# Attention, a squared-ReLU layer and a gated layer in one kernel: new numbers and rules for the planner that writes the order of the instructions

## The chip, the cores and the metric

The kernel runs on one core of a Trainium2 chip. Its time is the device time of one execution in microseconds (us), the median of several runs. One further execution was taken by the hardware profiler; all rows below are from it.

## The reference

Three layers follow each other, on 8 batches of 576 positions, 8 heads of 64 columns and 32 memory slots; the two feed-forward layers see 4608 tokens of 512 columns with 2048 hidden columns.

```python
# 1: attention through 32 slots
a = softmax(phi, axis=slots)                       # (b, h, s, 32), maximum subtracted
k_m = einsum('bhsm,bhsd->bhmd', a, k);  v_m = einsum('bhsm,bhsd->bhmd', a, v)
attn = softmax(q @ k_m.T / sqrt(64))               # (b, h, s, 32)
x = concat_heads(attn @ v_m)                       # 4608 x 512
# 2: first layer
r = maximum(x @ w_in, 0);  x = (s * r * r + b) @ w_out
# 3: second layer
h = x @ w1;  g = h * sigmoid(1.702 * h);  out = g @ w2
```

All is float32. The first weight matrix is not applied to x: `v_m @ w_in` is formed for each batch, 32 slots by 2048 columns per head, and attn is multiplied with that.

## The kernel before, in words

**Stages.** A plan lists the work in four stages. Stage 1, for each batch b: the slots of two groups of four heads (`slots`, written for g = 0 and 1), their attention weights (`attend`), four products of the slot values with a quarter of w_in (`matrix`, j = 0 to 3), and for each quarter four `step`s of twelve matmuls, each 128 x 288, whose ReLU goes to DRAM as r. Stage 2 multiplies the squares of r with w_out, one sequence s (a batch) after the other (`down` with "wo"). Stage 3 multiplies with w1 and gates (`up`), stage 4 multiplies with w2 (`down` with "w2"). Stages 2 to 4 use the seven-product scheme for 2 x 2 blocks: seven passes (numbers 1, 2, 6, 7, 5, 3, 4 in that order) accumulate in three PSUM tiles X, Y and Z, and sums and differences are formed on VectorE.

**Two halves.** Every operand of a matmul is split into a high part (a rounded copy) and a low part (the operand minus the copy), and three matmuls stand for one: high by high, high by low, low by high (lines 258 to 260, 602 to 604, 707 to 709). A high part is a copy on ScalarE or VectorE (lines 234 and 235); a low part is a subtraction on VectorE (line 239, shared by all such operations, so the tile names tell them apart: `ml` for `matrix`, `al` for attention weights, `ol` for stages 2 to 4).

**Weights** come as 64-bit floats. `convert` loads 512 KB (`raw`) and rebuilds a 32-bit number: two operations on ScalarE or VectorE (lines 278 to 287), three on VectorE (293 to 295: clamp, shift, sign), one addition on GpSimd (298). `prepare` does so for a quarter q of w_out, w1 or w2, forms the seven operands, splits each and stores it to DRAM; `weights` loads it when its stage comes. These stores and loads are called `w` in the trace's names.

**The maximum over the slots** in `slots` needs a path through three engines: VectorE reduces (line 404), TensorE transposes (412), VectorE reduces again to `nm` (413), TensorE transposes back (414), VectorE subtracts (409), ScalarE takes the exponential (416), TensorE multiplies with the keys and values (430, 432), VectorE normalizes to `an` (439 to 441), TensorE transposes it (447).

**The order** is not written by hand. Each operation is recorded with a due time, its possible engines with a cost in us, and the tiles it reads and writes. `Order.sort` is a list scheduler: at each turn it computes for every ready operation (among those due at most AHEAD after the most urgent one) when it could start: when its engine is free in the plan and its inputs were produced, plus LAG if on another engine. Each engine takes the earliest candidate, the due time deciding between equals, and the whole picks the earliest of the engines. The result is one fixed list per engine; at run time each engine goes through its list in order and waits on semaphores. All DMAs stand in the list of SyncE (SP). Wrong costs in the plan therefore do no harm to the results, only to the order. The relevant numbers are `LAG, FILL, AHEAD = 0.2, 2.5, 90.0` (line 36), `COL = 0.4527` ns for each column of a matmul (line 172), and B1, B2, the due-time length of a batch of stage 1 and of a sequence of the later stages (174). While the first batch is prepared, extra matmuls on an identity matrix (`warm`, line 747) fill the idle time that the plan sees on TensorE.

Of the kernel before, what the change touches and what calls it, by code (L numbers as in the profile page):

```python
# [27 lines left out]
class Order:  # L28
# [7 lines left out]
    LAG, FILL, AHEAD = 0.2, 2.5, 90.0  # L36
    WEIGHT = {"dve": 1.0, "pool": 1.6, "act": 1.0}

    def __init__(self, bufs):
        self.bufs, self.ops, self.fill = bufs, [], None  # L40
        self.wrote, self.read, self.users = {}, {}, {}

    def add(self, due, ways, r=(), w=()):
# [16 lines left out]
        self.ops.append((due, ways, deps, new))  # L60

    def sort(self):
        ops = self.ops
# [17 lines left out]
        ready = sorted((ops[n][0], n) for n in range(len(ops)) if not left[n])  # L81
        since = {n: 0.0 for _, n in ready}
        while ready:
            can = {}
            limit = ready[0][0] + self.AHEAD
            for due, n in ready:
# [32 lines left out]
            t, due, n, i = min(first)  # L119
            _, ways, _, new = ops[n]  # L120
            eng, cost, fn = ways[i]
# [7 lines left out]
            ready.remove((due, n))  # L129
            out.append(fn)  # L130
            for m in after[n]:
                left[m] -= 1
                if not left[m]:
                    bisect.insort(ready, (ops[m][0], m))
            for x in of[n]:
                last[x] = max(last[x], end[n])
                uses[x] -= 1
                if not uses[x]:
                    heapq.heappush(free[x[0]], last[x] + self.LAG)
# [5 lines left out]
class Net:  # L145
# [26 lines left out]
    COL = 0.4527  # L172

    B1, B2 = 38.5, 43.9
# [40 lines left out]
    def act(self, n, fn, psum=False, count=1):  # L215
        return "act", count * ((166 if psum else 195) + 0.835 * n) / 1e3, fn

    def dve(self, n, fn, fast=False, count=1):
        return "dve", count * (120 + (0.6 if fast else 1.06) * n) / 1e3, fn

    def pool(self, n, fn, fast=False):
        return "pool", (160 + (0.9 if fast else 2.6) * n) / 1e3, fn

    def pe(self, due, n, fn, r=(), w=()):
        self.order.add(due, [("pe", self.COL * n / 1e3, fn)], r, w)

    def dma(self, due, out, in_, r=(), w=(), kb=288):

        self.order.add(due, [("sync", kb / 340, lambda: self.nc.sync.dma_start(out(), in_()))], r, w)

    def hi(self, due, n, out, src, r, w, psum=False):
# [3 lines left out]
                             self.dve(n, lambda: nc.vector.tensor_copy(out(), src()), fast=not psum)], r, w)  # L235

    def tt(self, due, n, out, a, b, op, r, w, pool=False):
        nc = self.nc
        ways = [self.dve(n, lambda: nc.vector.tensor_tensor(out(), a(), b(), op=op))]  # L239
        if pool:  # L240
            ways.append(self.pool(n, lambda: nc.gpsimd.tensor_tensor(out(), a(), b(), op=op)))
        self.order.add(due, ways, r, w)

    def lo(self, due, n, out, src, hi, r, w, pool=False):

        self.tt(due, n, out, src, lambda: hi().bitcast(F32), ALU.subtract, r, w, pool)

    def on_act(self, due, n, fn, r=(), w=(), **k):
        self.order.add(due, [self.act(n, fn, **k)], r, w)

    def on_dve(self, due, n, fn, r=(), w=(), **k):
        self.order.add(due, [self.dve(n, fn, **k)], r, w)
# [10 lines left out]
    def convert(self, due, key, out, src, lead=6):  # L263
# [25 lines left out]
        def b():  # L289
            H, m = T[raw][:, :, 1], to["m"]  # L290
            mf = m.bitcast(F32)
            v = nc.vector
            v.tensor_scalar(mf, mf, bits(0x38000000), bits(0x47EFFFFF), op0=ALU.max, op1=ALU.min)
            v.tensor_scalar(m, m, 3, 0x3FFFFFF8, op0=ALU.logical_shift_left, op1=ALU.bitwise_and)
            v.scalar_tensor_tensor(m, H, 0xC0000000, m, op0=ALU.bitwise_and, op1=ALU.bitwise_or)
# [5 lines left out]
        for f, r, w in ((size, (*raw, 1), key), (low, (*raw, 1), (*raw, 0))):  # L301
            self.order.add(due, [self.act(512, lambda f=f: f(True)), self.dve(512, lambda f=f: f(False), fast=True)], (r,), (w,))
        self.on_dve(due, 512, b, ((*raw, 1),), (key,), fast=True, count=4)
        self.order.add(due, [("pool", 1.45, c)], ((*raw, 0),), (key,))
# [89 lines left out]
    def slots(self, b, g, due):  # L394
# [6 lines left out]
        self.dma(d - 8, lambda: self.t(ph, [P, 4, 5, 32]), lambda: self.a["phi"][b, g], (), (ph,), 320)  # L401
# [32 lines left out]
        self.pe(d + 4, 3600, mm, (ph, *fs, f1), (z,))  # L434
# [19 lines left out]
    def attend(self, b, g, due):  # L454
# [37 lines left out]
        self.on_dve(d + 2, S, lambda: with_slots(nc.vector, sm, ALU.subtract), (sm,), (st,))  # L492
        self.on_act(d + 3, S, lambda: nc.scalar.activation(T[st], T[st], AF.Exp, scale=0.125), (), (st,))
        self.on_dve(d + 4, S + 200, total, (st,), (sm2,))
        self.on_dve(d + 4, S, lambda: with_slots(nc.vector, sm2, ALU.mult), (sm2,), (st,))
# [6 lines left out]
    def matrix(self, b, j, due):  # L502
# [14 lines left out]
        self.pe(due, 5200, mm, (*kms, *[(*w, c) for w in ws for c in range(2)]), (pm,))  # L517
# [92 lines left out]
    def leave(self, name, s, i, z, due, X, Y, Z):  # L610
# [5 lines left out]

        def copy(k, half):

            if not scaled:
                self.on_act(due, n, lambda: nc.scalar.copy(self.two(k), T[X][:, :, 0:HS]), (X,), (k,), psum=True)  # L620
                return
            for o in range(2):
# [5 lines left out]
                self.on_act(due, HS + 100, f, (X, ("bw", 0), ("sc", 0, 0), *(((*k, 0),) if o else ())), ((*k, o),), psum=True)  # L628
# [266 lines left out]
```

## Time and profile before

| | us |
|---|---|
| median of 3 runs | 1498.03 (1495.05 to 1500.3) |
| the profiled execution | 1494.7 |
| its span, first to last instruction | 1492.9 |
| TensorE busy | 1414.1 (95%) |
| VectorE busy | 1198.5 (80%) |
| ScalarE busy | 775.0 (52%) |
| GpSimd busy | 96.2 (6%) |

Busy times are sums over the whole span; where the idle time of TensorE lies is read from a table by stretches of time, and what it waited for from the groups of instructions and from the timeline. TensorE's matmuls overlap: a 128 x 288 matmul is shown with about 0.3 us and the next one starts 0.13 us later. "PEclk" is the granted clock of TensorE as a share of 2.4 GHz.

### The profile page before, as it was taken

What the parts mean: (1) busy time and instruction counts of PE and PEld (TensorE: products, weight loads), DVE (VectorE), ACT (ScalarE), POOL (GpSimd) and SP (SyncE); (2) the same over time, 40 slices, a digit from 0 to 9 for tenths busy, and PEclk for the clock granted to TensorE, in tenths of its full rate; (3) what the DMA queues carried; (4) which work ended last, traced back from release to release, by engine and by line L of the source; (5) the groups of instructions that cost most, each with busy time, mean ns of one, the idle gap of its engine ahead of it and who ended that gap; (6) DMA issues with size and microseconds to landing.
All of it is one profiled execution on the core that took longest, in us unless ns stands there. A gap on an engine that the chain in (4) does not pass through costs nothing.

```text
span 1492.9 us, 28830 instructions
## 1 busy us (share of the span) xinstructions
PE 1414.1 (95%) x11192; PEld 1350.1 (90%) x11192; DVE 1198.5 (80%) x1836; ACT 775.0 (52%) x1244; POOL 96.2 (6%) x70
## 2 busy tenths in 40 slices
PE   7598899889999999999999999999999999999998
PEld 5476677767998999999999999999999999999998
DVE  6869888686799998998868888797649887778882
ACT  5345554436677767676545565564446433344431
POOL 1401110000101010100010101010000000000000
PEclk8699999999999999999999999999999999999999
DMA  9778988659885637564696575656389445444330
GB/s 349 241 249 297 346 307 309 237 183 339 319 289 184 218 125 261 186 234 156 211 353 227 190 268 189 252 186 236 117 311 363 143 124 152 144 143 127 108 117 32
DMA packets 136776, 329.20 MB, mean 221 GB/s; under 512 B 15552, under 2 KB 15552, under 8 KB 136640
## 3 DMA queue, kind: packets, MB, share of 16 engines
q1 hardware_dynamic: 136640, 327.37, 63.4%
q8 instruction: 88, 1.44, 0.4%
q14 instruction: 48, 0.39, 0.1%
HBM read 192.56 MB, written 134.74 MB: 219 GB/s over the span
## 4 chain that ended last, share of the span: by engine, by line
PE 57%; ACT 0%; DMA 0%; DVE 0%; issue 0%; SPq 0%
PE X L602 6%; PE X L604 6%; PE X L603 6%; PE X L707 5%; PE X L709 5%; PE X L708 5%; PE Y L602 3%; PE Y L604 3%; PE Y L603 3%; PE Y L707 2%; PE Y L709 2%; PE Y L708 2%; PE Z L602 2%; PE Z L604 2%; PE Z L603 2%; PE Z L707 1%
## 5 line engine op out<-in xcount | busy, mean ns | idle before, releaser
L260 PE MATMUL h<-ah,ml 128*128 128x288 f32 x512 | 156.1, 305 | 22.2 <-DVE ml L239 22.2
L258 PE MATMUL h<-ah,mh 128*128 128x288 f32 x512 | 162.5, 317 | 5.5 <-ACT mh L234 3.3
L602 PE MATMUL X<-oh,wo 128*128 128x288 f32 x512 | 153.7, 300 | 10.8 <-ACT u L626 9.0
L603 PE MATMUL X<-ol,wo 128*128 128x288 f32 x512 | 152.9, 299 | 2.6 <-DVE ol L239 2.6
L259 PE MATMUL h<-al,mh 128*128 128x288 f32 x512 | 155.3, 303 | 0.0
L602 PE MATMUL X<-oh,w 128*128 128x288 f32 x512 | 151.8, 296 | 0.7 <-ACT u L620 0.7
L604 PE MATMUL X<-oh,wo 128*128 128x288 f32 x512 | 151.9, 297 | 0.0
L707 PE MATMUL X<-oh,w 128*128 128x288 f32 x512 | 151.6, 296 | 0.0
L603 PE MATMUL X<-ol,w 128*128 128x288 f32 x512 | 151.0, 295 | 0.0
L708 PE MATMUL X<-ol,w 128*128 128x288 f32 x512 | 151.0, 295 | 0.0
L604 PE MATMUL X<-oh,w 128*128 128x288 f32 x512 | 150.5, 294 | 0.0
L709 PE MATMUL X<-oh,w 128*128 128x288 f32 x512 | 150.5, 294 | 0.0
L538 ACT ACTIVATE r<-h 128x576 f32<-128x576 f32 x121 | 78.3, 650 | 114.6 <-PE h L260 104.2
L258 PEld LDWEIGHTS h<-ah,mh 128*128 128x128 f32 x512 | 101.0, 197 | 27.2 <-issue 12.0
L260 PEld LDWEIGHTS h<-ah,ml 128*128 128x128 f32 x512 | 100.6, 196 | 24.4 <-DVE ml L239 24.4
L239 DVE TENSOR_TENSOR ol<-C,oh 128x576 fp32r<-128x576 f32 x128 | 96.3, 763 | 19.7 <-PE Y L603 9.6
L239 DVE TENSOR_TENSOR ol<-A,oh 128x576 fp32r<-128x576 f32 x128 | 97.4, 778 | 15.6 <-PE Y L603 8.0
L602 PEld LDWEIGHTS X<-oh,wo 128*128 128x128 f32 x512 | 97.3, 190 | 12.9 <-ACT u L626 10.8
L259 PEld LDWEIGHTS h<-al,mh 128*128 128x128 f32 x512 | 100.9, 197 | 0.0
L603 PEld LDWEIGHTS X<-ol,wo 128*128 128x128 f32 x512 | 97.4, 190 | 3.7 <-DVE ol L239 3.7
L604 PEld LDWEIGHTS X<-oh,wo 128*128 128x128 f32 x512 | 97.7, 191 | 0.0
L602 PEld LDWEIGHTS X<-oh,w 128*128 128x128 f32 x512 | 95.9, 187 | 1.2 <-ACT u L620 1.0
(183 smaller groups left out, 4251.0 us busy)
## 6 DMA issues: line engine op xcount, KB each, us to landing
w<-w SPq DMA_DIRECT2D x112, 512.0 KB, 5.1
r<-r SPq DMA_DIRECT2D x128, 288.0 KB, 3.6
g<-g SPq DMA_DIRECT2D x128, 288.0 KB, 2.4
wo<-wo SPq DMA_DIRECT2D x42, 512.0 KB, 5.0
kv<-in_kv SPq DMA_DIRECT2D x64, 258.0 KB, 4.9
raw<-in_w SPq DMA_DIRECT2D x32, 512.0 KB, 6.0
q<-in_q SPq DMA_DIRECT2D x32, 288.0 KB, 5.2
A<-r SPq DMA_DIRECT2D x32, 288.0 KB, 3.3
```

Of the source, the lines that this page charges most:

```text
L239: ways = [self.dve(n, lambda: nc.vector.tensor_tensor(out(), a(), b(), op=op))]
L258: self.nc.tensor.matmul(ps, wh, xh, start=start and i == 0, stop=False)
L259: self.nc.tensor.matmul(ps, wh, xl, start=False, stop=False)
L260: self.nc.tensor.matmul(ps, wl, xh, start=False, stop=(i == n - 1))
L538: self.act(2 * HS, lambda: nc.scalar.activation(self.two(r), T[h][:, :, 0:HS], AF.Relu), psum=True),
L602: nc.tensor.matmul(out, T[w][:, 0, c], T[h][:, p], start=f, stop=False, skip_group_check=True)
L603: nc.tensor.matmul(out, T[w][:, 0, c], T[l][:, p], start=False, stop=False, skip_group_check=True)
L604: nc.tensor.matmul(out, T[w][:, 1, c], T[h][:, p], start=False, stop=last, skip_group_check=True)
L707: nc.tensor.matmul(out, T[w][:, 0, c], T[h][:, k], start=f, stop=False, skip_group_check=True)
L708: nc.tensor.matmul(out, T[w][:, 0, c], T[l][:, k], start=False, stop=False, skip_group_check=True)
L709: nc.tensor.matmul(out, T[w][:, 1, c], T[h][:, k], start=False, stop=k == 1, skip_group_check=True)
```

## The change

- LAG, one number before, is now one for each receiving engine: 0.7 us before TensorE may start on another engine's output, 2.5 us when the receiver is a DMA, 0.25 us for the other three.
- Costs carry a flag for the port that VectorE and GpSimd share: while a flagged operation of the one runs in the plan, no flagged operation of the other may start. All GpSimd work and VectorE's operations between SBUF tiles are flagged. The three bit operations of `convert` become three separate entries.
- The cost of a column goes from 0.4527 to 0.463 ns; the costs of the matmuls in `slots`, `attend` and `matrix` are cut (3600 to 3000, 3000 to 2200, 5200 to 2600 columns). B2 goes from 43.9 to 44.8.
- AHEAD goes from 90 to 190. In stage 1 an engine takes the most urgent of the candidates that start within 0.3 us of the earliest (SLACK).
- The operations that read X, Y or Z out in stages 2 and 4 are ranked 100 us earlier than their due time (FIRST).
- `matrix` is due 8 us before its quarter instead of 4. The first slots, the first w_in pieces and their loads get other due times, so that the first loads interleave.
- The four quarters of w1 are prepared every 115 us instead of every 65 us.

No operation of the computation is added or removed.

```diff
-    LAG, FILL, AHEAD = 0.2, 2.5, 90.0
+    FILL, AHEAD, SLACK = 2.5, 190.0, 0.3
+    LAG = {"pe": 0.7, "sync": 2.5, "dve": 0.25, "act": 0.25, "pool": 0.25}
...
+        self.rank.append(due - first)
...
-                for i, (eng, cost, _) in enumerate(ways):
+                for i, (eng, cost, _, port) in enumerate(ways):
                     t = max(t0, at.get(eng, 0.0))
+                    if port:
+                        t = max(t, held["dve" if eng == "pool" else "pool"])
                     for d in deps:
-                        e = end[d] + (self.LAG if on[d] != eng else 0.05)
+                        e = end[d] + (self.LAG[eng] if on[d] != eng else 0.05)
...
-                first.append(min((c for c in v if c[0] <= t0), key=lambda c: c[1:]))
+                first.append(min((c for c in v if c[0] <= t0 + (self.SLACK if c[1] < self.until else 0.0)), key=lambda c: c[1:]))
...
+            if port:
+                held[eng] = t + cost
...
-    COL = 0.4527
+    COL = 0.463
+    FIRST = 100
-    B1, B2 = 38.5, 43.9
+    B1, B2 = 38.5, 44.8
...
-        self.pe(d + 4, 3600, mm, (ph, *fs, f1), (z,))
+        self.pe(d + 4, 3000, mm, (ph, *fs, f1), (z,))
...
-        self.pe(d, 3000, score, (*qs, km), (ps,))
+        self.pe(d, 2200, score, (*qs, km), (ps,))
...
-        self.pe(due, 5200, mm, (*kms, *[(*w, c) for w in ws for c in range(2)]), (pm,))
+        self.pe(due, 2600, mm, (*kms, *[(*w, c) for w in ws for c in range(2)]), (pm,))
...
-                    self.slots(0, g, -40 + 5 * g)
-                    self.attend(0, g, -26 + 5 * g)
+                    self.slots(0, g, -42 + 4 * g, 10)
+                    self.attend(0, g, -28 + 4 * g)
...
-                self.matrix(b, j, d - 4)
+                self.matrix(b, j, d - 8)
...
-            self.prepare("w1", q, t2 + 10 + 65 * q, step=4)
+            self.prepare("w1", q, t2 + 10 + 115 * q, step=4)
```

What this does to the lists is shown at three places. The first is VectorE's list in the first batch, up to `ml_436`, the low part of the first `matrix` (`raw` and `wi` belong to conversions of w_in, `st`, `a`, `aT`, `ah` and `al` to the attention weights). Before:

```order
L293 TENSOR_SCALAR wi_295<-wi_295 128x512
L294 TENSOR_SCALAR wi_295<-wi_295 128x512
L295 SCALAR_TENSOR_TENSOR wi_295<-raw_280,wi_295 128x512
L293 TENSOR_SCALAR wi_310<-wi_310 128x512
L294 TENSOR_SCALAR wi_310<-wi_310 128x512
L295 SCALAR_TENSOR_TENSOR wi_310<-raw_287,wi_310 128x512
L239 TENSOR_TENSOR ml_436<-vw_372,mh_393 128x1024
```

The same place now (the low part is `ml_404`; lines are numbered by the changed file, where 247 is the old 239):

```order
L505 STREAM_TRANSPOSE aT_383<-st_313 128x576
L242 CAST ah_387<-aT_383 128x576
L247 TENSOR_TENSOR al_391<-aT_383,ah_387 128x576
L299 TENSOR_SCALAR wi_289<-wi_289 128x512
L302 SCALAR_TENSOR_TENSOR wi_289<-raw_249,wi_289 128x512
L296 TENSOR_SCALAR wi_289<-wi_289 128x512
L247 TENSOR_TENSOR ml_404<-vw_299,mh_323 128x1024
```

The first `ml` stood at row 61 of VectorE's list behind nine finished conversions of w_in, and stands at row 55 behind five finished ones and the clamp of a sixth. Four of those five now stand ahead of the first attention weights, where before only the first operation of one stood.

The second place is TensorE's list around the two transposes of the slot maximum in a later batch (`s<-ident,an` is the first, `s<-ident,nm` the second). Before:

```order
L260 MATMUL h_1503<-ah_971,ml_1400 128x288
L412 MATMUL s_1526<-ident,an_1135 128x128
L414 MATMUL s_1545<-ident,nm_1539 128x128
L515 MATMUL vw_1553<-wi_277,km_1132 32x512 x2
L515 MATMUL vw_1553<-wi_295,km_1132 32x512 x2
```

Now (first rows of it):

```order
L421 MATMUL s_1512<-ident,an_1128 128x128
L263 MATMUL h_1524<-ah_1381,mh_1444 128x288
L264 MATMUL h_1524<-al_1385,mh_1444 128x288
L265 MATMUL h_1524<-ah_1381,ml_1508 128x288
L263 MATMUL h_1524<-ah_1491,mh_1444 128x288
```

The second transpose, which stood right behind the first at four places of stage 1, now stands 24 matmuls of two steps behind it here, and at least one `vw` product behind it everywhere after the first batch. In the same list the first step that uses a `matrix` stood 12 matmuls behind it in 24 of 32 cases and 48 in seven; now it is 36 or 48 in 28 cases, while the first four cases, all in the first batch, have 0, 0, 0 and 12 (before 0, 12, 12, 12).

The third place is SP's list where stage 3 begins. `w_6_3` is the DRAM copy of piece 6 of quarter 3 of w1, `w_3_3` that of piece 3; `w_1722` and `w_1736` are the tiles that TensorE reads; `g` are stores of stage 3's output, `w_4_0` belongs to w2. Now:

```order
L236 DMA w_6_3_9740<-w_1689_9584 128x1024
L236 DMA w_4_0_9758<-w_1681_9538 128x1024
L236 DMA g_2_1_1_9779<-g_9714 128x576
L236 DMA w_1722_9799<-w_6_3_9740 128x1024
L236 DMA g_2_0_1_9820<-g_9734 128x576
L236 DMA w_3_3_9825<-w_1713_9738 128x1024
L236 DMA g_2_1_0_9834<-g_9776 128x576
L236 DMA g_3_0_0_9855<-g_9805 128x576
L236 DMA w_1736_9873<-w_3_3_9825 128x1024
```

Before, the same two pieces were stored at rows 492 and 497 of this list and loaded at rows 567 and 575; now they are stored at rows 584 and 589 and loaded at 587 and 592. The number at a name's end counts tiles in the order of the plan. Between the store 9740 and the first matmul on `w_1722` TensorE's list has some four blocks of twelve matmuls, and about as many between the store 9825 and the first on `w_1736`. For piece 7 it is seven blocks.

## Rows read from the trace of the kernel before

**Rows 1.** Stretches: length; busy PE, PEld, DVE, ACT, POOL; PEclk; DMA share; GB/s.

```profile
0.00:49.90 49.90, 29.39 (x257) 22.21 (x257) 36.96 (x64) 24.66 (x40) 13.74 (x15) 0.79 0.94 326
49.90:90.00 40.10, 33.65 (x313) 27.30 (x314) 32.40 (x53) 14.80 (x22) 9.66 (x8) 0.88 0.79 273
90.00:375.00 285.00, 252.75 (x2467) 206.81 (x2465) 227.08 (x385) 140.47 (x218) 22.21 (x16) 0.97 0.80 280
375.00:720.00 345.00, 330.55 (x2408) 326.81 (x2407) 309.50 (x459) 236.79 (x396) 25.62 (x16) 0.98 0.64 220
720.00:1488.00 768.00, 767.27 (x5753) 766.80 (x5752) 591.78 (x878) 358.27 (x568) 24.95 (x16) 1.00 0.55 189
```

**Rows 2.** Timeline, VectorE, first 50 us: start, duration, instruction, idle time before.

```profile
18.34 0.43 DVE L280 TENSOR_SCALAR wi<-raw 128x512 uint32<-128x512 uint32 x1 [2.26 <-DMA raw<-in_wi]
18.69 0.84 DVE L478 STREAM_TRANSPOSE st<-a 128x288 f32<-128x288 f32 x2
...
35.20 0.36 DVE L293 TENSOR_SCALAR wi<-wi 128x512 f32<-128x512 f32 x1
...
37.33 1.51 DVE L293 TENSOR_SCALAR wi<-wi 128x512 f32<-128x512 f32 x1
...
48.62 1.22 DVE L239 TENSOR_TENSOR ml<-vw,mh 128x1024 fp32r<-128x1024 f32 x1
```

**Rows 3.** Timeline, GpSimd, same stretch.

```profile
36.88 1.68 POOL L298 TENSOR_TENSOR wi<-wi,raw 128x512 uint32<-128x512 uint32 x1 [1.94 <-DVE wi L295]
```

**Rows 4.** Timeline, TensorE, the first low part.

```profile
49.90 0.61 PE L260 MATMUL h<-ah,ml 128*128 128x288 f32 x1 [11.74 <-DVE ml L239]
```

**Rows 5.** Groups on TensorE, 90 to 375 us: busy, mean ns, idle before and releaser.

```profile
L258 PE MATMUL h<-ah,mh 128*128 128x288 f32 x432 | 135.9, 314 | 4.4 <-ACT mh L234 2.2 <-ACT r L538 1.2 <-DVE ml L239 1.0
L260 PE MATMUL h<-ah,ml 128*128 128x288 f32 x431 | 130.0, 302 | 8.6 <-DVE ml L239 8.6
...
L515 PE MATMUL vw<-wi,km 64*32 64x512 f32 x448 | 31.9, 626 | 0.0
L472 PE MATMUL a<-q,km 64*32 64x288 f32 x192 | 13.9, 405 | 0.0
L430 PE MATMUL s<-kv,ph 128*32 128x129 f32 x384 | 13.1, 276 | 0.0
...
L447 PE MATMUL s<-ident,an 128*128 128x128 f32 x12 | 3.5, 295 | 4.3 <-DVE an L441 4.3
L414 PE MATMUL s<-ident,nm 128*128 128x128 f32 x12 | 3.5, 292 | 14.9 <-DVE nm L413 14.9
```

**Rows 6.** Timeline, TensorE, a `vw` and a slot product.

```profile
156.60 1.09 PE L515 MATMUL vw<-wi,km 64*32 64x512 f32 x16
157.62 1.09 PE L430 MATMUL s<-kv,ph 128*32 128x129 f32 x32
...
158.99 0.40 PE L258 MATMUL h<-ah,mh 128*128 128x288 f32 x1
```

**Rows 7.** Timeline, TensorE, after a long wait for `nm`.

```profile
140.60 0.29 PE L414 MATMUL s<-ident,nm 128*128 128x128 f32 x1 [4.17 <-DVE nm L413]
...
142.40 0.44 PE L259 MATMUL h<-al,mh 128*128 128x288 f32 x1
142.64 0.44 PE L260 MATMUL h<-ah,ml 128*128 128x288 f32 x1
```

**Rows 8.** Groups on VectorE, 90 to 720 us.

```profile
L239 DVE TENSOR_TENSOR ml<-vw,mh 128x1024 fp32r<-128x1024 f32 x28 | 34.1, 1216 | 9.7 <-ACT mh L234 9.4
```

**Rows 9.** Groups on ScalarE, 90 to 720 us.

```profile
L234 ACT CAST mh<-vw 128x1024 fp32r<-128x1024 f32 x24 | 24.2, 1010 | 6.2 <-PE vw L515 6.2
```

**Rows 10.** Groups on TensorE, 375 to 720 us.

```profile
L602 PE MATMUL X<-oh,wo 128*128 128x288 f32 x451 | 135.7, 301 | 10.8 <-ACT u L626 9.0 <-ACT a L626 1.6
L603 PE MATMUL X<-ol,wo 128*128 128x288 f32 x451 | 134.9, 299 | 2.6 <-DVE ol L239 2.6
```

**Rows 11.** DMA issues: count, KB each, median us to landing.

```profile
w<-w SPq DMA_DIRECT2D x112, 512.0 KB, 5.1
```

More of the change, by code (lines that the diff above doesn't have):

```diff
@@ L28, with add @@
 class Order:
[L36 removed]
+    FILL, AHEAD, SLACK = 2.5, 190.0, 0.3
+    LAG = {"pe": 0.7, "sync": 2.5, "dve": 0.25, "act": 0.25, "pool": 0.25}
     WEIGHT = {"dve": 1.0, "pool": 1.6, "act": 1.0}
     def __init__(self, bufs):
[L40 removed]
+        self.bufs, self.ops, self.rank, self.fill, self.until = bufs, [], [], None, 0
         self.wrote, self.read, self.users = {}, {}, {}
[L43 removed]
+    def add(self, due, ways, r=(), w=(), first=0):
         n = len(self.ops)
@@ L80, in sort @@
                 of[n].append(x)
-        ready = sorted((ops[n][0], n) for n in range(len(ops)) if not left[n])
+        held = {"dve": 0.0, "pool": 0.0}
+        ready = sorted((rank[n], n) for n in range(len(ops)) if not left[n])
         since = {n: 0.0 for _, n in ready}
@@ L117, in sort @@
                 t0 = min(v)[0]
-                first.append(min((c for c in v if c[0] <= t0), key=lambda c: c[1:]))
-            t, due, n, i = min(first)
+                first.append(min((c for c in v if c[0] <= t0 + (self.SLACK if c[1] < self.until else 0.0)), key=lambda c: c[1:]))
+            t, _, n, i = min(first)
             _, ways, _, new = ops[n]
-            eng, cost, fn = ways[i]
+            eng, cost, fn, port = ways[i]
+            if port:
+                held[eng] = t + cost
             if self.fill and eng == "pe":
@@ L234, in hi, with tt, lo, on_act @@
         self.order.add(due, [self.act(n, lambda: nc.scalar.copy(out(), src()), psum),
-                             self.dve(n, lambda: nc.vector.tensor_copy(out(), src()), fast=not psum)], r, w)
-    def tt(self, due, n, out, a, b, op, r, w, pool=False):
+                             self.dve(n, lambda: nc.vector.tensor_copy(out(), src()), fast=not psum, port=not psum)], r, w)
+    def tt(self, due, n, out, a, b, op, r, w, first=0):
         nc = self.nc
[L239 to L252, printed above, removed]
+        port = not any(k[0] == "ps" for k in r)
+        self.order.add(due, [self.dve(n, lambda: nc.vector.tensor_tensor(out(), a(), b(), op=op), port=port)], r, w, first)
+    def lo(self, due, n, out, src, hi, r, w):
+        self.tt(due, n, out, src, lambda: hi().bitcast(F32), ALU.subtract, r, w)
+    def on_act(self, due, n, fn, r=(), w=(), first=0, **k):
+        self.order.add(due, [self.act(n, fn, **k)], r, w, first)
+    def on_dve(self, due, n, fn, r=(), w=(), first=0, **k):
+        self.order.add(due, [self.dve(n, fn, **k)], r, w, first)
     def mm3(self, ps, pairs, start=True):
@@ L301, in convert @@
         for f, r, w in ((size, (*raw, 1), key), (low, (*raw, 1), (*raw, 0))):
-            self.order.add(due, [self.act(512, lambda f=f: f(True)), self.dve(512, lambda f=f: f(False), fast=True)], (r,), (w,))
-        self.on_dve(due, 512, b, ((*raw, 1),), (key,), fast=True, count=4)
-        self.order.add(due, [("pool", 1.45, c)], ((*raw, 0),), (key,))
+            self.order.add(due, [self.act(512, lambda f=f: f(True)), self.dve(512, lambda f=f: f(False), fast=True, port=True)], (r,), (w,))
+        self.on_dve(due, 512, clamp, (), (key,), fast=True, port=True)
+        self.on_dve(due, 512, shift, (), (key,), fast=True, port=True)
+        self.on_dve(due, 512, sign, ((*raw, 1),), (key,), port=True)
+        self.order.add(due, [("pool", 1.35, c, True)], ((*raw, 0),), (key,))
     def prepare(self, name, q, due, keep=False, step=1.5):
@@ L615, in leave @@
         scaled = name == "wo"
+        first = self.FIRST
         def copy(k, half):
             if not scaled:
-                self.on_act(due, n, lambda: nc.scalar.copy(self.two(k), T[X][:, :, 0:HS]), (X,), (k,), psum=True)
+                self.on_act(due, n, lambda: nc.scalar.copy(self.two(k), T[X][:, :, 0:HS]), (X,), (k,), first, psum=True)
                 return
@@ L764, in plan @@
         t2 = B * B1
+        self.order.until = t2
         t3, t4 = t2 + B * B2, t2 + 2 * B * B2
```

50 lines of the change are left out of this document (24 added, 26 removed).

## The prediction

> **What bounds the kernel now.** I read the table by stretches first, with one question: where is TensorE not at its full rate? From 720 us to the end it starts 5753 matmuls in 768 us, one every 0.1335 us, at PEclk 1.00 [rows 1]. Nearly all of them are 128 x 288, so 0.1335 us is the price of one such matmul, and nothing can be won there without removing matmuls. Every loss lies ahead of 720 us:
>
> - 0 to 49.9 us, the preparation of the first batch. TensorE's own work is small here. VectorE is busy 37.0 of 49.9 us [rows 1]. The stretch ends when the first low part `ml` is there: TensorE had waited 11.74 us for it [rows 4], and VectorE only began it at 48.62 us [rows 2].
> - 90 to 375 us, stage 1 from its second batch on, 285 us. Work at the full rate: 3 x 432 matmuls x 0.1335 = 173 us (three lines of this count); 28 `vw` products of 16 instructions at 1.02 us (the distance of their starts) = 28.6; 12 slot products at 1.37 = 16.4; at most 13.9 for the scores; some 4 for 36 transposes, an estimate [rows 5, 6]. That is 236 us, so 49 us are lost. The groups show 32.2 us of them as waits: 14.9 for `nm`, 4.3 for `an`, 13.0 ahead of the `h` matmuls, 11.8 of these for `mh` and `ml` [rows 5]. The rest is slow running: PEclk is 0.97 [rows 1], and after a wait of 4.17 us the matmuls start 0.24 us apart instead of 0.13, which is the lower of the two clock levels [rows 7].
> - 375 to 720 us, the end of stage 1 and most of stage 2: 2408 matmuls x 0.1335 = 321.5 of 345 us, so 23.5 us are lost [rows 1]; 13.4 are shown as waits ahead of X's matmuls, 10.8 of them for the copy that empties X on ScalarE [rows 10].
>
> VectorE is no bound over the whole span, but it is near one: 227 of 285 us (80%) in the second stretch, 309.5 of 345 (90%) in the third [rows 1].
>
> **The change part by part.** The sum is made against the profiled execution: span 1492.9, time 1494.7. The median of the runs is 1498.0, 3.3 above it.
>
> *(a) The first batch: -6.* Four conversions now stand ahead of the first attention weights, where VectorE had been waiting for data until 18.34 us [rows 2]. At most VectorE's 12.9 us of idle time come back. Against this, the loads of q stand behind four more pieces of 512 KB: at the 326 GB/s of this stretch [rows 1] that is 6.4 us later for the attention weights, which began at 18.69 us [rows 2]. The port rule helps too: a clamp of 0.36 us took 1.51 when it started behind a running GpSimd addition of 1.68 [rows 2, 3]. I take 9 us back. Then the second and third `matrix` have no matmuls left between themselves and their first user where they had twelve: 2 x 12 x 0.1335 = 3.2 us of cover gone. Bounds: -12.9 and +6.4.
>
> *(b) Stage 1 from the second batch: -28.* At four places the two transposes of the slot maximum stood back to back, so TensorE waited for VectorE to reach the reduction in its list; these make up the 14.9 us. After each some twelve matmuls run at the low clock, 12 x (0.24 - 0.1335) = 1.3 us, so 20 us in all. Now a `vw` (1.02 us) or at least a step of twelve matmuls (1.6 us) stands between. Five places have only the `vw`; I leave them 0.5 us each: -17.5. For `mh` and `ml`: a copy takes 1.01 us and the subtraction 1.22 [rows 8, 9], 2.2 us without handoffs, against 12 x 0.1335 = 1.6 us of cover before and 36 x 0.1335 = 4.8 us now. What is left over, 2.6 us, is what VectorE may be behind. Of the 11.8 us I let 1.3 stay: -10.5. The waits for `an` (4.3) keep their distances and stay. VectorE's work is the same, 227 us; in 257 us it fills 88%, near to the 90% at which the third stretch runs. Bounds: -46, all but 3 us of the loss gone and VectorE 95% full; -8, half of what the four transposes cost given back later.
>
> *(c) Stage 2: -4.* The copies of X are ranked earlier, the distances to matmuls are larger in the plan, and a quarter of w1's preparation leaves the stage. But VectorE remains at about 90%, and TensorE's list now has five places in stage 2 where the next pass into X stands directly behind the last one, where it had three. Bounds: -15 (the 13.4 us and some slow clock) and +8 (the 10.8 us grow as the places do, by five thirds).
>
> *(d) Where stage 3 begins: +5.* This is a new wait. The last quarter of w1 is prepared 150 us later, and its pieces are loaded directly behind their own stores. A transfer `w` of 512 KB takes 5.1 us to land [rows 11], so a store and the load behind it take 10.2 us. For pieces 6 and 3 four blocks of twelve matmuls cover 6.4 us of that. Piece 6 comes 3.8 us late; that delay covers piece 3, and 1.3 us go to the low clock. On SP both loads hold up what is queued behind them, stores of `g` and a store for w2, which nobody needs soon. Bounds: 0 (the stores land faster with fewer transfers around them) and +36 (the third rival).
>
> The Trainium skill ("DMA: Bandwidth & Descriptors", section "Anatomy of one DMA — SWDGE (gpsimd) path") gives a transfer 2.0 us plus its bytes at 436 GB/s, fitted on another issuing path than SP's: 3.2 us for 512 KB as an estimate, where this trace has 5.1. By that rule store and load take 6.4 us, all covered, (d) is 0 and the sum five lower; I go by the row.
>
> From 720 us on nothing is to be had, and the late part of the preparation falls where VectorE has room: 592 of 768 us [rows 1].
>
> Sum: -6 - 28 - 4 + 5 = -33; 1494.7 - 33 = 1461.7, say 1462.
>
> **The rivals.**
>
> *VectorE's list sets stage 1.* Then a wait that is removed at one transpose turns up at the next operation that VectorE is late with. For it: 90% in the third stretch goes with 23.5 us of loss on TensorE. Against it: in the second stretch it idles 58 of 285 us. Price: (b) is -12 and (c) -2: 1494.7 - 6 - 12 - 2 + 5 = 1480.
>
> *Nearly all goes.* (a) -12, (b) -46, (c) -15, (d) 0: 1422. For it: every listed wait is one of distance, and work is there to fill it. Against it: VectorE would have to run 95% full.
>
> *Slower: the last quarter of w1 comes late, one piece after the other.* Pieces 7, 6, 5 and 3 are each stored and loaded close together, and SP takes them in order, so a load that waits for its store holds up the next store. If all four chains run in series, 4 x 10.2 = 41 us, less 3 x 24 matmuls (9.6 us) between their users, plus four times 1.3 us of low clock: +36. With (b) at -8, (a) -6, (c) -4 the time is 1513. It decides once (d) is over 38 us with the other terms as forecast, or over 18 with these. Against it: pieces 7 and 5 have more cover, seven blocks for piece 7.
>
> *The plan is only permuted.* The order is another one, but its errors against the chip are as large elsewhere: within 4.5 us of before.
>
> **How the numbers follow.** Forecast 0.60, VectorE's list 0.17, nearly all 0.12, permuted 0.05, slower 0.06. A measurement tells about 0.3% (4.5 us) from no change. Faster: 0.60 + 0.17 + 0.12 = 0.89; same 0.05; slower 0.06. The range reaches from the middle between the second rival and the forecast's own low side, 1434, to 1487, above the first rival's 1480. The forecast's own range is 1445 to 1474.
>
> **What the profile will show.** (a) The first matmul on `ml` at about 43 us instead of 49.9. (b) The idle time before the second transpose under 4 us in all, that for `ml` and `mh` after the first batch under 4 us, and PEclk at 0.99 in that stretch; VectorE at 87% or more. (c) The wait for the copies of X still at 6 to 10 us. (d) One or two waits of TensorE for a transfer of `w` when stage 3 begins, some 4 us. The forecast is wrong if stage 1 from its second batch to its last `h` is less than 15 us shorter, if the waits reappear behind other operations of VectorE, or if TensorE waits over 15 us for w1.

## The result and the profile after

The changed kernel takes 1441.27 us (median of four runs, 1438.53 to 1444.89); the kernel before, on the same chip, 1496.76 (four runs). The ratio is 0.9628, 95% interval [0.9597, 0.9658]: 3.7% faster, where 2.4% were forecast (1462). The profiled execution took 1444.89, 49.8 us less than the one of before. I cut both traces at two events: the first `h` matmul of the second batch (all of the first batch lies ahead of it) and the last `h<-ah,mh` matmul (stage 1 ends).

| stretch, us | before | after | change |
|---|---|---|---|
| start to the second batch's first `h` | 97.0 | 83.1 | -14.0 |
| from there to the last `h` | 292.6 | 256.9 | -35.7 |
| from there to the end of the span | 1103.3 | 1103.1 | -0.2 |

All of the gain is in stage 1. The same stretches as [rows 1], with the columns named there, shifted to where the same work now stands:

```profile
0.00:38.15 38.15, 24.90 (x255) 20.09 (x255) 28.96 (x58) 18.51 (x29) 7.22 (x11) 0.94 0.98 351
38.15:80.00 41.85, 39.46 (x358) 32.15 (x359) 37.17 (x66) 20.77 (x32) 14.92 (x11) 0.89 0.93 335
80.00:325.00 245.00, 239.94 (x2394) 195.49 (x2393) 217.03 (x371) 139.26 (x218) 21.68 (x16) 0.99 0.90 315
325.00:670.00 345.00, 334.59 (x2468) 331.47 (x2467) 288.82 (x444) 234.42 (x392) 22.31 (x12) 0.99 0.64 213
670.00:1438.00 768.00, 764.46 (x5719) 763.64 (x5718) 605.55 (x896) 363.57 (x577) 29.90 (x20) 1.00 0.57 196
```

In the third row TensorE is busy 98% of the time (89% in [rows 1]) at PEclk 0.99 (0.97), and VectorE 89% (80%). The last row has one matmul every 0.1343 us (0.1335 before), 4.6 us more over its 5719; the waits for w1 shown below lie in it. TensorE's groups, 80 to 325 us, which answer [rows 5]:

```profile
L263 PE MATMUL h<-ah,mh 128*128 128x288 f32 x418 | 129.4, 309 | 2.9 <-DVE ah L242 2.9
L264 PE MATMUL h<-al,mh 128*128 128x288 f32 x418 | 124.0, 297 | 1.2 <-DVE al L247 1.2
L265 PE MATMUL h<-ah,ml 128*128 128x288 f32 x418 | 123.8, 296 | 0.7 <-DVE ml L247 0.6
...
L423 PE MATMUL s<-ident,nm 128*128 128x128 f32 x12 | 3.6, 297 | 0.3 <-DVE nm L422 0.2
L456 PE MATMUL s<-ident,an 128*128 128x128 f32 x12 | 3.5, 290 | 0.0
```

32.2 us of waits have become 5.1: `nm` 14.9 to 0.3, `ml` 8.6 to 0.7, `an` 4.3 to 0.0. What is left is new, `ah` and `al`, the next batch's attention weights. The first low part, which answers [rows 4] and the last row of [rows 2]; timeline, TensorE, then VectorE:

```profile
38.15 0.61 PE L265 MATMUL h<-ah,ml 128*128 128x288 f32 x1 [6.53 <-DVE ml L247]
```

```profile
22.59 0.85 DVE L487 STREAM_TRANSPOSE st<-a 128x288 f32<-128x288 f32 x2 [0.88 <-PE a L481]
...
36.88 1.22 DVE L247 TENSOR_TENSOR ml<-vw,mh 128x1024 fp32r<-128x1024 f32 x1
```

The attention weights begin 3.9 us later than before, yet the low part begins 11.7 us earlier. Behind stage 1, TensorE's groups from 340 us to the end (the first answers [rows 10]) and the timeline where stage 3 begins:

```profile
L611 PE MATMUL X<-oh,wo 128*128 128x288 f32 x512 | 154.4, 301 | 10.4 <-ACT u L637 10.2
L612 PE MATMUL X<-ol,wo 128*128 128x288 f32 x512 | 153.2, 299 | 0.0
...
L718 PE MATMUL X<-oh,w 128*128 128x288 f32 x512 | 152.3, 297 | 2.6 <-DMA w<-w 2.6
```

```profile
755.03 0.37 PE L718 MATMUL Y<-oh,w 128*128 128x288 f32 x1 [0.25 <-DMA w<-w]
...
761.01 0.58 PE L718 MATMUL X<-oh,w 128*128 128x288 f32 x1 [2.56 <-DMA w<-w]
```

X's copies are waited for as long as before (10.2 us, 10.6 before), the waits for `ol` are gone, and two waits for w1 are new. The median landing of `w` is now 5.7 us ([rows 11] had 5.1):

```profile
w<-w SPq DMA_DIRECT2D x112, 512.0 KB, 5.7
```

### The profile page after: what moved, and what is told of

It reads as the page before. It is cut to its first block, busy times and chain, and to the rows that moved or that the text cites. A ratio compares the mean times of both kernels' runs of the same rounds, so it can differ in the third digit from the quotient of the medians.

```text
span 1443.1 us, 28776 instructions
## 1 busy us (share of the span) xinstructions
PE 1404.1 (97%) x11190; PEld 1343.4 (93%) x11190; DVE 1178.3 (82%) x1833; ACT 776.5 (54%) x1247; POOL 96.0 (7%) x70
## 4 chain that ended last, share of the span: by engine, by line
PE 85%; DVE 7%; DMA 5%; ACT 2%; issue 1%; SPq 0%; DVEq 0%; ACTq 0%
PE X L611 9%; PE X L613 9%; PE X L612 9%; PE X L718 5%; PE X L719 5%; PE X L720 5%; PE Y L611 4%; PE Y L613 4%; PE Y L612 4%; PE h L263 4%; PE h L265 4%; PE h L264 4%; PE Y L718 2%; PE Z L611 2%; PE Y L720 2%; PE Y L719 2%
## 5 line engine op out<-in xcount | busy, mean ns | idle before, releaser
L611 PE MATMUL X<-oh,wo 128*128 128x288 f32 x512 | 154.4, 301 | 10.4 <-ACT u L637 10.2
L247 DVE TENSOR_TENSOR ol<-C,oh 128x576 fp32r<-128x576 f32 x128 | 94.9, 753 | 21.3 <-ACT oh L241 10.9
L247 DVE TENSOR_TENSOR ol<-A,oh 128x576 fp32r<-128x576 f32 x128 | 95.8, 766 | 17.9 <-PE X L613 4.4
L611 PEld LDWEIGHTS X<-oh,wo 128*128 128x128 f32 x512 | 97.9, 191 | 12.5 <-ACT u L637 12.5
L265 PEld LDWEIGHTS h<-ah,ml 128*128 128x128 f32 x512 | 98.5, 192 | 10.5 <-DVE ml L247 10.5
L241 ACT CAST oh<-A 128x576 fp32r<-128x576 f32 x109 | 70.2, 673 | 68.7 <-PE Y L613 29.7
```

Of the source, the lines that this page charges most:

```text
L241: self.order.add(due, [self.act(n, lambda: nc.scalar.copy(out(), src()), psum), self.dve(n, lambda: nc.vector.tensor_copy(out(), src()), f ...
L247: self.order.add(due, [self.dve(n, lambda: nc.vector.tensor_tensor(out(), a(), b(), op=op), port=port)], r, w, first)
L265: self.nc.tensor.matmul(ps, wl, xh, start=False, stop=(i == n - 1))
L611: nc.tensor.matmul(out, T[w][:, 0, c], T[h][:, p], start=f, stop=False, skip_group_check=True)
```

## The experiments

The first number of each result is the time as a share of that of the kernel before on the same chip, with its 95% interval. "First" is the time of the second batch's first `h`, "rest" the stretch from there to the last `h`, "end" what follows. All from the profiled runs; before has 97.0, 292.6, 1103.3, the changed kernel 83.1, 256.9, 1103.1. Differences of a few us in "end" come with every new order, as the table at the end of this section shows. Each stretch is from one execution, and that is up to 5.9 us off the median of its kernel (SLACK in the kernel before: 1499.4 against 1493.5; the changed kernel: 1444.9 against 1441.3), so a difference of a few us between two runs is not settled by them.

**Before, with `matrix` due 8 us ahead.**

```diff
-                self.matrix(b, j, d - 4)
+                self.matrix(b, j, d - 8)
```

> The kernel before with one number changed: matrix is due 8 us before its quarter instead of 4. Theory of distance (stage 1 lost time because too few matmuls stood in TensorE's list between a product and the operations of other engines on it): 24 of 32 cases go from 12 matmuls to 36 or more, and two of the four back-to-back pairs of transposes get a vw between them, so from the second batch's first h to the last h it takes 262 us instead of 292.6, and the time is 1466. Rival, the port (VectorE came late because its plan ignored GpSimd): at most 8 us go, 1489. Rival, the handoff times LAG: also at most 8, 1489.

Measured 0.9891 [0.9861, 0.9920]; first 93.9, rest 281.3. That is 11.3 of the 35.7 us, more than the rivals' 8 and far less than the theory's 30. It is not the cover for `mh` and `ml` alone: two of the four pairs of transposes are parted too. In this stretch the waits for `mh` and `ml` fall from 12.5 to 2.5 us, those for `an` (4.3) go, `nm` still costs 9.6 us in 3 waits, and 5.9 us of waits for `ah` and `al` are new.

**Before, with the LAG of the change.**

```diff
-    LAG, FILL, AHEAD = 0.2, 2.5, 90.0
+    FILL, AHEAD = 2.5, 90.0
+    LAG = {"pe": 0.7, "sync": 2.5, "dve": 0.25, "act": 0.25, "pool": 0.25}
...
```

> The kernel before with the new LAG alone (0.7 us ahead of TensorE, 2.5 for DMAs, 0.25 for the others). In the order four pairs of transposes stay back to back, and the cover behind matrix stays at 12 to 24 matmuls for half of the cases. Theory of distance: 10 us go, 1487. Rival LAG: 25 us go, 1472. Rival port: nothing goes, 1496.

Measured 0.9958 [0.9943, 0.9973]; first 92.8, rest 283.8, end 1111.1. In stage 1 the waits for `ml` nearly go (8.6 us before), those for `nm` grow (14.9 before); TensorE's waits, 92 to 377 us (who waited for what: us in total, times, longest):

```profile
PE s L415 <- DVE nm L414: 21.8, 4, 5.8
PE h L261 <- DVE ml L240: 1.7, 1, 1.7
```

So a larger distance in the plan did not part the two transposes.

**After, with `matrix` due 4 us ahead** (the first diff reversed, in the changed kernel).

> The changed kernel with matrix due 4 us ahead again, everything else as changed. In the order 17 cases after the first batch fall back to 12 to 24 matmuls. Theory of distance: 15 to 20 us come back, 1458. Rivals port and LAG: 0 to 5, 1444.

Measured 0.9676 [0.9642, 0.9709]; first 86.1, rest 262.7: 5.8 us back in the rest, where 15 to 20 or at most 5 were expected. TensorE's waits are now nearly all for `ml`, 10.9 us in 6 between 80 and 350 us.

**After, without the port rule.**

```diff
-                    if port:
-                        t = max(t, held["dve" if eng == "pool" else "pool"])
```

> The changed kernel whose plan does not hold flagged operations back for each other (the port is ignored, all else as changed). The distances behind matrix and between the transposes stay as large; the first ml moves from row 55 to 65 of VectorE's list. Theory of distance: some 5 us come back in the first batch and 0 to 3 in the rest of stage 1, 1447. Rival port: 20 us or more come back over stage 1, 1461 or more.

Measured 0.9676 [0.9649, 0.9703]; first 91.95, rest 256.1. The rule is worth 8.9 us, all in the first batch; timeline, TensorE:

```profile
45.86 0.61 PE L263 MATMUL h<-ah,ml 128*128 128x288 f32 x1 [13.46 <-DVE ml L245]
```

The stalls are back on the shift of w_in's conversion (VectorE's group, this kernel first, then the changed one):

```profile
L297 DVE TENSOR_SCALAR wi<-wi 128x512 uint32<-128x512 uint32 x16 | 14.6, 912 | 0.4
```

```profile
L299 DVE TENSOR_SCALAR wi<-wi 128x512 uint32<-128x512 uint32 x16 | 8.3, 519 | 0.1
```

Without the rule the first low part comes 7.7 us later (45.86 against 38.15). Three shifts ahead of it take 1.38 to 1.40 us instead of 0.42, 2.9 us together; and eight finished conversions stand ahead of it in VectorE's list instead of five, 3 x (0.42 + 0.42 + 0.69) = 4.6 us. So the rule acts by the order as well as by the stalls.

**After, with SLACK 0.** The two transposes stand back to back again at several places.

```diff
-    FILL, AHEAD, SLACK = 2.5, 190.0, 0.3
+    FILL, AHEAD, SLACK = 2.5, 190.0, 0.0
```

> The changed kernel with SLACK at 0 (the earliest start decides, the due time only between equals), all else as changed. In its order four pairs of slot transposes stand back to back again, as before, and the cover behind matrix stays at 36 or more. Theory now (two distances): SLACK is what put matmuls between the transposes, so a wait for nm of some 4 us comes back at four places with the low clock behind it; from the second batch's first h to the last h it takes 275 us instead of 256.9, the time is 1459. Rival (VectorE's backlog came from the rest of the planner's numbers, which stay): waits for nm under 1.5 us each, 1446.

Measured 0.9619 [0.9581, 0.9657]; first 83.9, rest 257.4, end 1092.4. The theory of distances, on which the larger part of my term (b) rests, fell here: the pairs are there and cost little. The four of this stretch wait 0.47, 0.76, 0.43 and 0.38 us, where the four of before waited 4.17, 4.27, 2.59 and 3.92. Timeline, TensorE, the third of them, and VectorE beside it:

```profile
235.51 0.33 PE L421 MATMUL s<-ident,an 128*128 128x128 f32 x1
236.26 0.32 PE L423 MATMUL s<-ident,nm 128*128 128x128 f32 x1 [0.43 <-DVE nm L422]
```

```profile
235.55 0.46 DVE L242 CAST ah<-aT 128x576 fp32r<-128x576 f32 x1
235.92 0.28 DVE L422 TENSOR_REDUCE nm<-s 128x1 f32<-128x128 f32 x1
```

VectorE takes up the reduction 0.4 us after the first transpose began. Before, at 136.17 us, it took it up at 140.20, because it was still at work that stood ahead in its list. Timeline of the kernel before, TensorE, then VectorE:

```profile
136.17 0.27 PE L412 MATMUL s<-ident,an 128*128 128x128 f32 x1
```

```profile
135.75 0.74 DVE L485 TENSOR_REDUCE a<-st 128x18 f32<-128x576 f32 x1
136.53 0.18 DVE L486 TENSOR_SCALAR a<-a 128x18 f32<-128x18 f32 x1
136.74 0.27 DVE L487 RECIPROCAL a<-a 128x18 f32<-128x18 f32 x1
136.92 0.63 DVE L239 TENSOR_TENSOR swo<-cwo,cwo 128x512 f32<-128x512 f32 x1
137.46 0.74 DVE L481 TENSOR_TENSOR st<-st,a 128x576 f32<-128x576 f32 x1
138.37 1.23 DVE L239 TENSOR_TENSOR ml<-vw,mh 128x1024 fp32r<-128x1024 f32 x1 [0.16 <-ACT mh L234]
139.51 0.77 DVE L496 STREAM_TRANSPOSE aT<-st 128x576 f32<-128x576 f32 x1
140.20 0.25 DVE L413 TENSOR_REDUCE nm<-s 128x1 f32<-128x128 f32 x1
```

So the wait of 4.17 us [rows 7] is VectorE running late on seven other operations, not the way from engine to engine. The other three waits are of the same kind: in each of the four VectorE is idle for at most 0.23 us.

**Before, with SLACK 0.3.** The transposes are parted in the old plan.

```diff
-    LAG, FILL, AHEAD = 0.2, 2.5, 90.0
+    LAG, FILL, AHEAD, SLACK = 0.2, 2.5, 90.0, 0.3
...
-                first.append(min((c for c in v if c[0] <= t0), key=lambda c: c[1:]))
+                first.append(min((c for c in v if c[0] <= t0 + (self.SLACK if c[1] < self.until else 0.0)), key=lambda c: c[1:]))
```

> The kernel before with SLACK 0.3 in stage 1 added and nothing else. In its order no pair of transposes is back to back (at least one step of twelve matmuls between), the cover behind matrix is 12 to 24 matmuls in 26 cases, as before. Theory of two distances: the waits for nm go (20 us with the low clock), those for ml stay or grow: second batch to last h 274 us instead of 292.6, time 1477. Rival: the backlog only shows elsewhere, 288 us and 1491.

Measured 0.9985 [0.9965, 1.0005]: no change. Rest 292.8, as before. The wait moved; TensorE's waits, 85 to 380 us:

```profile
PE h L261 <- DVE ml L240: 20.1, 13, 3.4
PE s L448 <- DVE an L442: 3.9, 4, 1.5
```

`nm` (14.9) is gone and `ml` (8.6) has 20.1, though the cover behind `matrix` is nearly as before (12 matmuls in 26 cases, 24 before): at the four longest of these waits `mh` was ready 3.1 to 6.6 us before VectorE began `ml`. This is the first rival of the prediction, VectorE's list, in its pure form, and the mirror image of the run above.

**Before, with SLACK 0.3 and `matrix` 8 us ahead.**

> The kernel before with SLACK 0.3 in stage 1 and matrix due 8 us ahead, nothing else. Both distances are then nearly those of the changed kernel (at least a vw between the transposes, at least 36 matmuls behind matrix but for the first). Theory of two distances: second batch to last h 262 us, close to the changed kernel's 256.9; the first batch stays as before; time 1466. Rival (costs, LAG and the port are needed too): 275 us or more, 1478.

Measured 0.9878 [0.9850, 0.9906]; first 95.8, rest 277.0. Together 15.6 us, as the rival said; `ml` still costs 9.6 us in 4 waits.

**After, with the old due times of the first loads.**

```diff
-                    self.slots(0, g, -42 + 4 * g, 10)
-                    self.attend(0, g, -28 + 4 * g)
+                    self.slots(0, g, -40 + 5 * g)
+                    self.attend(0, g, -26 + 5 * g)
...
-                        self.convert(9.6 * j - 24 + 2 * c, (*k, c % 2), make, self.a["wi"][4 * j + c], 24 - 2 * c if j == 0 else 6)
+                        self.convert(9.6 * j - 24 + 2 * c, (*k, c % 2), make, self.a["wi"][4 * j + c])
```

> The changed kernel with the first slots, attention weights and w_in pieces at their old due times and leads. Only the first batch's order changes. If the interleaved first loads gave the 14 us that the first batch won (first h of the second batch at 83 us instead of 97), that h comes at 95 us and the time is 1453. Rival: the other numbers give it, since the first ml stays at row 53 of VectorE's list; then it comes at 86 us or less, and the time is 1444.

Measured 0.9667 [0.9635, 0.9699]; first 87.8, rest 258.6: the loads give 4.8 us, in the first batch; neither 95 nor 86 us came.

**Before, with the plan's numbers of the change**: the two diffs above for LAG and `matrix`, and

```diff
-    COL = 0.4527
+    COL = 0.463
-    B1, B2 = 38.5, 43.9
+    B1, B2 = 38.5, 44.8
-        self.pe(d + 4, 3600, mm, (ph, *fs, f1), (z,))
+        self.pe(d + 4, 3000, mm, (ph, *fs, f1), (z,))
...
-        self.pe(d, 3000, score, (*qs, km), (ps,))
+        self.pe(d, 2200, score, (*qs, km), (ps,))
...
-        self.pe(due, 5200, mm, (*kms, *[(*w, c) for w in ws for c in range(2)]), (pm,))
+        self.pe(due, 2600, mm, (*kms, *[(*w, c) for w in ws for c in range(2)]), (pm,))
```

> The kernel before with four sets of the changed numbers: the costs of TensorE's work (COL, B2 and the three cut costs of slots, attend and matrix), LAG, and matrix due 8 us ahead. SLACK, the port, the split of convert, AHEAD, FIRST, the first loads and w1 stay as before. Theory now (the plan's clock: before, the plan gave TensorE some 6 us too much per batch, so VectorE was planned later than TensorE needed it; the right costs keep VectorE on time): second batch to last h 262 us or less instead of 292.6, time 1467 or less. Rival (the order of VectorE's own list: the one-piece convert bunches VectorE's work, whatever TensorE costs): 275 us or more, 1479.

Measured 0.9824 [0.9810, 0.9839]; first 95.6, rest 268.9. Neither figure came, neither 262 nor 275. With no new rule, 23.7 of the 35.7 us are there, but only 1.4 of the 14 in the first batch. Beside the run with `matrix` alone (281.3) the other numbers give 12.4.

**After, with clamp, shift and sign as one entry again.**

```diff
-        self.on_dve(due, 512, clamp, (), (key,), fast=True, port=True)
-        self.on_dve(due, 512, shift, (), (key,), fast=True, port=True)
-        self.on_dve(due, 512, sign, ((*raw, 1),), (key,), port=True)
+        def three():
+            clamp(), shift(), sign()
+
+        self.on_dve(due, 512, three, ((*raw, 1),), (key,), fast=True, count=4, port=True)
```

> The changed kernel with the three bit operations of convert planned as one piece again (flagged for the port, cost as before), all else as changed. Theory of the plan's clock: second batch to last h stays within 4 us of 256.9, time 1443. Rival (one-piece convert bunches VectorE's work and holds it up): 268 us or more, 1453.

Measured 0.9675 [0.9658, 0.9692]; first 89.8, rest 255.2, end 1097.3. The first batch loses 6.7 us, though its first low part comes a little earlier (36.98 us); the rest loses nothing.

**After, with all the old numbers** (the diff of COL, B2 and the three costs reversed) and

```diff
-    LAG = {"pe": 0.7, "sync": 2.5, "dve": 0.25, "act": 0.25, "pool": 0.25}
+    LAG = {"pe": 0.2, "sync": 0.2, "dve": 0.2, "act": 0.2, "pool": 0.2}
```

> The changed kernel with the old numbers of the plan (column 0.4527 ns, B2 43.9, the three old matmul costs, 0.2 us to every engine); what stays is the port rule, SLACK, the three entries, the first loads, `matrix` 8 us ahead. Theory 'bunches': what costs time in stage 1 is a stretch of TensorE's list with more VectorE work beside it than VectorE can do; counted from the lists, VectorE's largest running backlog in stage 1 is 16.7 us before, 10.0 after, 14.2 to 17.9 in the slow variants (269 to 293 us from the second batch's first h to the last h), 8.6 to 13.2 in the fast ones (255 to 263). Here it is 10.4, so that stretch should take at most 263 us although all the numbers are old; with some waits for w1 (one of its loads stands next to its use) a time of 1440 to 1456. Theory 'plan's clock': the numbers set it; that stretch is 270 us or more and the time 1458 to 1480.

Measured 0.9777 [0.9756, 0.9797], 1462.9 us; first 88.9, rest 266.2. Both theories missed that stretch: the bunches wanted at most 263, the plan's clock 270 or more (its time, 1458 to 1480, did come). Taken from the changed kernel, these numbers are worth 9.3 us in the rest (12.4 when given to the old one) and 5.8 in the first batch. Two lines of TensorE's waits over the whole span follow, the second where w1 is late; the 16.3 us of the first hold one wait of 6.5 in the first batch:

```profile
PE h L265 <- DVE ml L247: 16.3, 9, 6.5
...
PE Y L718 <- DVE w L247: 5.8, 1, 5.8
```

**A version with SLACK 0 and w1 every 100 us**: the SLACK diff above, and

```diff
-            self.prepare("w1", q, t2 + 10 + 115 * q, step=4)
+            self.prepare("w1", q, t2 + 10 + 100 * q, step=4)
```

> The changed kernel with SLACK 0 and w1 prepared every 100 us instead of 115. Stage 1 as with SLACK 0 alone (257 us), no wait for w1 when stage 3 begins (2.6 us after the change), X's copies at most 8 us: 1432 to 1438, faster than the changed kernel by 0.3 to 0.6%. If what SLACK 0 showed from the last h on (1092 instead of 1103 us) was luck of that order, it is 1440 to 1448.

Measured 0.9591 [0.9573, 0.9609], 1435.31 us (four runs, 1434.47 to 1435.73), all of them below the lowest run of the changed kernel (1438.53); the intervals of the two ratios overlap a little. From SLACK 0 alone (1437.42, its runs from 1433.91 to 1442.43) it can't be told apart. First 84.7, rest 257.4, end 1091.7. Where the 11.4 us in "end" between the two profiled executions come from shows in PEclk; stretches of the changed kernel, then of this one (columns as in [rows 1]):

```profile
460.00:470.00 10.00, 9.99 (x63) 9.95 (x64) 6.39 (x9) 5.77 (x10) 1.31 (x1) 0.83 0.56 165
600.00:610.00 10.00, 7.04 (x44) 6.81 (x43) 6.75 (x11) 6.29 (x11) 0.00 (x0) 0.85 0.77 254
650.00:660.00 10.00, 9.97 (x63) 9.97 (x64) 7.45 (x12) 5.98 (x10) 0.00 (x0) 0.83 0.59 184
760.00:770.00 10.00, 8.99 (x57) 9.02 (x58) 5.92 (x11) 4.05 (x7) 0.00 (x0) 0.83 0.96 343
```

```profile
460.00:470.00 10.00, 8.10 (x57) 7.62 (x57) 8.26 (x12) 8.48 (x16) 1.71 (x1) 1.00 0.89 293
...
600.00:610.00 10.00, 10.00 (x77) 10.00 (x76) 9.45 (x15) 9.45 (x16) 0.00 (x0) 1.00 1.01 364
650.00:660.00 10.00, 9.24 (x69) 9.01 (x69) 8.37 (x12) 6.32 (x11) 1.31 (x1) 1.00 0.88 282
...
760.00:770.00 10.00, 10.00 (x77) 10.00 (x76) 4.26 (x7) 4.85 (x8) 0.00 (x0) 1.00 0.94 329
```

In two of these stretches the changed kernel starts 63 matmuls, all of the time busy, where 10 / 0.1335 = 75 are possible; from 340 us on, such stretches of 10 us cost it 6.8 us in sum ((1 - PEclk) x 10 over those below 0.985), this version 0.8. The waits for X's copies, `ol` and w1 are 8.7 us instead of 13.8, the longest 1.7 instead of 3.0, and none for w1 is left. Together 5.1 + 6.0 = 11.1 of the 11.4 us.

**Stage 1 from its second batch, side by side.** "Bunch" is an estimate, worked out from the lists with the trace's mean durations: the largest running excess of VectorE's work over TensorE's, when both lists are cut at the same operations.

| kernel | rest, us | bunch, us | end, us |
|---|---|---|---|
| before, SLACK | 292.8 | 17.9 | 1106.1 |
| before | 292.6 | 16.7 | 1103.3 |
| before, LAG | 283.8 | 16.7 | 1111.1 |
| before, `matrix` | 281.3 | 14.4 | 1105.8 |
| before, SLACK and `matrix` | 277.0 | 14.2 | 1104.5 |
| before, all numbers | 268.9 | 16.3 | 1102.7 |
| after, all old numbers | 266.2 | 10.4 | 1102.4 |
| after, old `matrix` | 262.7 | 13.2 | 1096.6 |
| after, old loads | 258.6 | 11.5 | 1101.3 |
| after, SLACK 0 | 257.4 | 12.4 | 1092.4 |
| after | 256.9 | 10.0 | 1103.1 |
| after, no port rule | 256.1 | 12.6 | 1099.2 |
| after, one entry | 255.2 | 8.6 | 1097.3 |

## Why the prediction was right, and where it was not

The sign, the place (stage 1) and the range were right; the median of 1441.27 lies below the forecast's own range of 1445 to 1474. Point by point, on the profiled executions:

- **(a), the first batch: -6 forecast, -14.0 measured**, 1.1 us beyond the bound of -12.9. The step that failed is "at most VectorE's 12.9 us of idle time come back": it took VectorE's work ahead of the first `ml` as fixed. 11.7 of the 14.0 us lie ahead of that low part (its matmul starts at 38.15, where I had 43), and there VectorE's idle time fell only from 12.9 to 9.2 us, its work from 37.0 to 29.0 ([rows 1] and the first row that answers it). Four finished conversions fewer stand ahead, and the clamp of one more: 4 x (0.42 + 0.42 + 0.69) - 0.42 = 5.7 us. And before, five clamps and a shift ahead of `ml` took 0.76 to 1.52 us; now the longest takes 0.62, 4.7 us less in sum. I had named such stalls, with no term of their own. Without the port rule the first batch is 8.9 us longer. The later attention weights were there (3.9 us, I had 6.4); the low part came earlier all the same.
- **(b), stage 1 from the second batch: -28 forecast, -35.7 measured**, inside the bounds, but the step "the two transposes of the slot maximum stood back to back, so TensorE waited" has the wrong cause. Parting them in the old plan gained nothing (292.8), and putting them together in the new one cost nothing (257.4). What is shown is that VectorE was late at these places. The forecast came out near because the waits did go, nearly all of them: between the two events from 33.0 to 4.9 us, and the low clock, (1 - PEclk) x length, from 10.2 to 1.7. That is 28.1 + 8.5, about the 35.7; I had 22.9 and 5.2. Of the waits that I left standing (4.3 for `an`, whose distance stayed, 2.5 for `nm`, 1.3 for `ml`) hardly any is left, against 4.1 us of new ones for `ah` and `al`. VectorE's work between these events is 227.7 us before and 222.4 after; I had kept it equal. At 86% of VectorE (89% in the window shown) the waits did not come back: the first rival's limit was not one.
- **Term (b)'s part for `mh` and `ml`**: the lead of 8 us alone gave 11.3 us, with 10.5 forecast, but that they are near is partly luck. The waits for these two did fall by 10.0 us; in that run the waits for `an` and 5.3 us of those for `nm` went too, and 5.9 us of others came. Nor is the cover the whole cause, since with SLACK in the old plan the waits for `ml` doubled at nearly the same cover.
- **(c) -4 and (d) +5, together +1; -0.2 measured.** Cut at stage 3's first matmul, and with 0.1335 us for each matmul, TensorE loses 21.5 us in stage 2 before and 16.9 after, and 5.0 and 9.4 behind it: by this estimate (c) is -4.6 and (d) +4.4, both sized right. The gain of (c) is not where I looked for it: X's copies are waited for 10.2 us (10.6 before; sign forecast: 6 to 10), and what went is 2.6 us for `ol` and smaller pieces. (d) was right in kind: two waits, 2.8 us, and 1.7 us of low clock in 760 to 770, 4.5 in all. Piece 6's store took 8.7 us to land and its load 4.0, where I had 10.2 for both. The rival in which w1's last quarter comes in series did not come: piece 3's store and load took 5.1 and 4.4 us, and TensorE did not wait for it.
- **By the Trainium skill's rule** ("DMA: Bandwidth & Descriptors", "Anatomy of one DMA — SWDGE (gpsimd) path"), a fit for another path than SP's, a store and a load would take 6.4 us, an estimate, and (d) would be 0. The row has 5.7 us for one transfer, and the waits are there, so the measurement decides against carrying the rule over to SP's path.

**What sets the 35.7 us.** No single part. Along one path of runs they fall into three nearly equal steps: `matrix` earlier 11.3 (292.6 to 281.3), the other numbers of the plan 12.4 (to 268.9), and what is left, the port rule, SLACK, the three entries, the first loads and a GpSimd cost that went from 1.45 to 1.35 us, 12.0 (to 256.9). AHEAD, FIRST and the distance of w1's quarters have no part in it: with their old values the changed plan gives the same list for every engine up to the end of stage 1. In the other order, rules before numbers, the last two are 15.1 (281.3 to 266.2) and 9.3. Of the third step no part has a price of its own in this stretch when it is taken away: loads 1.7, port rule, SLACK and three entries between -1.7 and 0.5, all within what one execution differs from another. So it looks as if they stand in for each other; no run takes away two or three of them together. The size of VectorE's bunches puts the kernels nearly in order, but not two of them: 268.9 goes with a bunch of 16.3 and 266.2 with 10.4. That VectorE was late where TensorE waited is shown; that bunches in its list are the whole cause is only argued. How the second step divides between LAG and the costs of matmuls stays open, since with `matrix` they were run only together. What AHEAD and FIRST do behind stage 1 was not tried alone.

## What to carry to other kernels

A wait on a short reduction or copy is not a matter of distance until the other engine's own row shows that it was free: look at what it did in that time. If it was busy with other work, parting the two instructions can just move the wait to its next customer, as it did here. What went with the gain here, with two exceptions in the table, is a list in which its work is spread more evenly beside the bound engine's. Several rules of a planner can stand in for each other, so that each is worth next to nothing when it alone is taken away and all of them 12 us, as in the rest of stage 1 here; run the sum as well as the parts.

## What was not expected of the hardware

- Two transposes with VectorE's reduction between them, one right behind the other on TensorE, cost 0.43 us of wait when VectorE took the reduction next (at 235.5 us of the run with SLACK 0) and 4.17 us when seven other operations came first.
- VectorE's busy time fell by 20 us between the two kernels (1198.5 to 1178.3) at nearly the same count of instructions (1836 and 1833), the clamps and shifts beside GpSimd's additions among the shorter ones. Yet without the port rule only the first batch became longer, by 8.9 us; the rest of stage 1 stayed (256.1).
- From the last `h` on, two profiled executions of the same work in another order differ by 11.4 us, more than half of it in the clock: stretches of 10 us at PEclk 0.83 to 0.85 became stretches at 1.00. How much of this the order sets is open. The medians of the two kernels are 6.0 us apart, and one order, SLACK 0 alone, took 1433.9 to 1442.4 us in four executions, at mean clocks of 0.996 to 0.991.
